# An S5 scan and a Hedgehog attention in one kernel: K's weight in halves, a block of x transposed on TensorE, and a new order of steps

## The chip, the cores and the metric

The kernel runs on one core of a Trainium2 chip. The metric is the device time of one execution in microseconds (us). A core has five engines, each with its own queue of instructions that it takes strictly in order: TensorE (PE; its weight loads are shown apart as PEld), VectorE (DVE), ScalarE (ACT), GpSimd (POOL) and SyncE (SP), which issues transfers. ScalarE and GpSimd issue transfers too. TensorE writes into eight PSUM banks, and VectorE or ScalarE copies ("evacuates") a bank to SBUF before it is used again.

## The reference

From an input x of 2048 tokens by 512 features two branches are computed and mixed by a gate:

```
g = sigmoid((x * gate_w).sum(-1))
# A: a diagonal complex state space with 512 states
h_t = Lam_bar * h_{t-1} + B_bar x_t                a = 2 Re(C h_t) + x * Dskip
# B: linear attention, 32 heads of 16, feature map = softmax(+) beside softmax(-)
q, k, v = x @ wqkv
phi(u) = [softmax(u @ w_phi), softmax(-u @ w_phi)]
b = (phi(q) (phi(k)^T v) / (phi(q) sum(phi(k)) + 1e-6)) @ wo
out = g * a + (1 - g) * b
```

Inputs and output are bf16, and sums are in f32.

## The kernel before

The 2048 tokens are sixteen tiles of 128. Tile `ti` holds the tokens with remainder `ti // 4` modulo 4 within a quarter `ti % 4` of 512 tokens: the scan runs four tokens at a step, so a tile is one phase of one quarter. `xT` holds x with features on partitions; `x_load` (line 224) fills a tile of it by a transposing transfer from HBM on SP's queue, eight tiles first, then B's matrices plain and transposed (`Bn_r`, `Bn_i`, `BrT`, `BiT`), the other eight tiles, Q's weight transposed (`WTq`), C's matrices and `Wo`.

The head-wise map `w_phi` is folded into the weights of K and Q. `st_B` makes a block-diagonal matrix `BD` from `Wc` (w_phi) and a mask. `st_W` (line 278) transposes K's weight on TensorE, four 128 x 128 blocks at a time, into `WTk`; `st_f` multiplies by `BD` and writes K's folded weight `Wk2`. `st_w` does the same for Q.

For each tile, `st_k` and `st_v` are four matmuls each (128 x 128 weights, 512 columns), whose result goes to `Xq` or to one of eight buffers `vx`. For each pair of tiles the feature map follows: `x` (a tree of four maxima and a subtraction), `n` (the same with minima), `e` (two exponentials on ScalarE), `s` (a tree of four sums, then ln and exp on ScalarE, then a product on VectorE). `st_a` accumulates phi(k)^T v in two PSUM banks over all tiles, and the gate's sums with it. For Q the same comes in pairs `A`, `B` and in groups of four tiles, `X1`..`S3`, whose results four transposing transfers on SP bring into `phT`.

The state space: `V`, `U`, `P`, `P2` to `P4`, `M` compute its parameters from three vectors (`vec_n`), which GpSimd loads and TensorE transposes in `V`; `i0`..`i3` make sine and cosine tables, `D` diagonal matrices `dg`, `p` and `g` the inputs of the scan, `z0`..`z3` the scan itself on VectorE (ten steps each), `h`, `c`, `K`, `r`, `b` what the output needs. The output of tile n is `y` (state and direct part), `o` (attention: matmuls, ln and exp on ScalarE, two products on VectorE, a transposing transfer) and `t` (`Wo`, the gate, the store).

All functions `st_*` are generators, and the order of the whole kernel is written out by hand in the string `ORDER` (line 24). Each token runs one generator to its next `yield`. `k1@3` is the first part of `k1` with PSUM bank 3; `W1:D` has its evacuation on VectorE instead of ScalarE; `t4:A` issues its store from ScalarE's queue; `F:36` issues 36 matmuls on a constant tile, whose result nobody reads. The block is a manual schedule for PE, DVE, ACT and SP (line 152): each of them gets its instructions in the order in which the tokens issue them. Waits between engines are added for the data; so are waits for buffers that are used again. GpSimd's order is chosen by the framework.

Of the kernel before, what the change touches and what calls it, by code (L numbers as in the profile page):

```python
# [10 lines left out]
ALU = mybir.AluOpType  # L11
AX = mybir.AxisListType
# [12 lines left out]
B B F:36 W2@0 W2 W1@1 W1:D W0@2 W0:D W3@3 B W3 B F:8 f3@4 F:1 V@5 V f3 f0@6 f2@7 P f0 U P f2 P2 f1@0 U f1 v1@1 P2 v2@2  # L25
k1@3 k0@5 P2 P2 U V2@4 k5@6 k3@7 P P2 P4 P4 U P4 i0 k2@0 P3 P2 P3 k1 i0 k7@3 i1 i0 k0 i0 i0 v1 i2 i1 x0 x0 k4@5 i1 n0
k3 x0 i1 M v2 V2 v7@1 n0 i2 k2 k7 v3@4 i1 i3 x0 n0 x0 i3 k4 k5 v4@7 i2 n0 i2 k6@2 i2 x1 n0 i3 x1 v0@0 i3 D v4 v3 p22@3
x1 n1 v5@5 p00@6 x1 n1 x1 i3 x2 L n1 x2 p30@7 v7:D e0 p20@4 x2 D v5 n1 n1 p10@1 p20 n2 p02@5 p30 p10 x2 e0 D n2 s0 v0
v6@4 k6 g101@7 p00 x2 s0 x3 n2 s0 g001@1 g000@0 n2 s0 e1 e1 g001 n2 s1 s0 s0 e2 g100@2 p22 g101 g001 x3 n3 gw s0 e2 n3
k9@6 x3 v6 g100 a0@31 k9 g000 a0 s1 n3 s1 n3 k8@4 g000 x3 s1 s1 s1 g100 k10@6 s2 k8 x3 n3 p12@0 e3 g101 k11@2 s1 e3 x4  # L30
k11 a1 s2 g010@4 n4 k10 a1 s2 g011@7 n4 x4 s2 n4 x4 n4 s3 g010 g011 s2 x4 s3 x4 n4 x5 k12@2 s3 p02 s2 e4 n5 k13@6 x5
e4 s3 x5 s2 n5 s3 g010 g011 s4 a2 k12 g011 x5 n5 s3 p32@5 k13 s4 n5 a2 s3 x5 n5 x6 g010 z0 s4 w0@2 n6 w0 p32 v9@7 w3@6
z0 g111@4 p12 g210@2 n6 w3 s4 e5 e5 w1@5 s5 w1 a3 v8@0 x6 k14@6 s4 z0 g111 g110@5 a3 n6 z0 v9 s5 v8 k15@7 k14 s4 v11@0
z0 x6 x6 z0 k15 s4 n6 w2@6 g110 w2 g201@7 x6 g111 g111 x7 g110 z0 a4 x7 c01@6 z0 g200@4 g110 z1 s5 q1@5 v11 z1 g311@0
s5 x7 s5 n6 s5 c01 n7 g201 e6 z1 g211@6 a4 z1 g201 x7 g200 v10@7 z1 z1 e6 g200 z0 g210 q0@4 g211 g210 s5 q1 n7 v12@5
q0 q3@4 x7 n7 s6 z0 g210 n7 s6 n7 g211 s6 v10 nA xA g301@2 s6 a5 e7 z1 g300@7 g211 q3 e7 nA v14@6 z1 xA z2 nA q2@4 v14
a5 z2 g300 xA s6 s7 q2 z2 s6 s7 z2 g301 g300 xA s7 g311 g301 v12 g310@6 xA g311 z1 nA c11@4 z1 nA eA z2 nB s7 z2 c03@7
c12@2 g310 xB g311 eA q15@5 c12 s6 c03 s7 g310 h01@0 nB q15 g310 sA c10@2 z2 s7 h01 c11 c13@7 xB nB v13@5 z3 xB h11@6
z2 c10 z3 a6 z2 sA z2 h11 q9@0 c02@4 v13 sA q9 xB a6 nB c13 h10@2 q6@5 c02 v15@0 z3 q12@7 q10@6 q8@4 xB v15 sA nB
h21@0 q12 z3 h00@7 q6 q10 q5@5 eB q8 s7 q4@6 a7 sA eB q4 z3 z3 h10 z3 c00@4 q7@2 c00 a7 sB sA r1 sB z3 sB z3 h20@6 sA  # L40
K0@4 sB q7 sA sB z3 q13@2 q5 h31@5 h21 q14@0 sB G h20 h30@6 sA sB h00 q13 h31 sA sB sB sB G h30 Y q11@2 END N1 K2@7 X1
Y o0@5 N1 o1@6 r0 K0 o1 Y X1 N1 X1 q11 Y o0 X1 N1 o0@3 X1 N1 o0 o1@4 y1@1 o1 q14 o1 o0 b1 o0 N2 y0@2 o2@0 o0 K2 X2 o0
E1 o1 E1 E1 y1 E1 o2 X2 K3@7 N2 X2 o2@5 o1 y0 o1 y2@3 S1 o2 o2 o2 K1@6 K1 y2 S1 o2 S1 N2 X2 o2 S1 y3@4 o3@0 y0 r1 X2
N2 K3 S1 S1 N2 y3 r0 S1 S1 S1 o3 o3@5 o3 G y1 y3 y7@6 o3 E2 t0 y2 o3 E2 E2 E2 G t1 o3 t0 y5@7 t2 N3 y4@0 t2 y7 b1 X3
r3 o4@5 N3 S1 S2 S2 o4 o4@2 y5 b0 o4 o4 t1 o3 y4 o4 o5@3 o5 o4 b0 S1 o5@5 S2 t3 o5 b3 S1 o5 r2 o5 y4 y6@1 t3 r2 o4 y7
o6@2 t1 b2 S2 r3 o6 o6@3 y6 b2 o7@4 o6 S2 t0 o5 y5 y6 o5 t4 o6 b3 o7 S2 S2 t2 y8@5 o6 X3 o6 S2 y11@2 t4 X3 t4:A o7@0
o7 N3 y10@3 X3 o7 o6 N3 y11 t5 y10 X3 N3 o7 t6 o7 S2 E3 y8 S2 o8@4 E3 E3 o8 o8@0 o8 S2 o8 o7 t5:D t6:D o8 o8 y10 y8
y9@7 o10@1 o9@4 E3 o9 S3 o9@0 S2 o9 o10 o8 o9 o9 y9 S3 t7 S3 o9 t6 o10@4 y11 o9 o10 S3 o10 y9 o10 S3 o10 y14@0 t8 t7
y13@1 S3 S3 t5:A o11@4 y12@6 y13 o11 t8 o10 S3 o11@5 o11 t9 S3 t9:D S3 y14 t3:A o11 t10 o12@7 o11 S3 o11 t10:D o12
o12@4 o12 o12 y14 o12 o13@5 S3 o13 o13@3 y12 o12 o13 t7 t8:A o13 o11 o13 o12 o14@7 o14 o14@4 o13 o14 t9:A y13 o14 y12  # L50
o14 o14 o15@5 o15 o15@3 y15@7 o15 o15 t11 o15 t11 o13 o14 o15 y15 t12 y15 t10 t12 t14 t14 o15 t11 t12 t13 t14:A t15
t15 t13:D t15:A t13
# [16 lines left out]
def kernel(  # L69
# [29 lines left out]
    ORD = (3, 1, 0, 2)  # L99
    KVW = 4 * (Dh + 1)  # L100
# [61 lines left out]
    nc.scalar.dma_start(out=wk_nat[:], in_=B_wqkv[:, D:2 * D].rearrange("(k p) n -> p k n", p=P))  # L162
    nc.scalar.dma_start(out=Wc[:], in_=B_w_phi.rearrange("(k hl) e f -> (hl e) k f", hl=8))
    nc.scalar.dma_start(out=Wv[:], in_=B_wqkv[:, 2 * D:3 * D].rearrange("(k p) n -> p k n", p=P))
# [19 lines left out]
    K0T = const.tile([P, KT, D], BF16, name="K0T")  # L184
# [42 lines left out]
    for ti in range(8):  # L227
        x_load(ti)
# [5 lines left out]
    for ti in range(8, NTI):  # L234
        x_load(ti)
# [26 lines left out]
    mask16 = stg.tile([P, 8], F32, name="mask16", bufs=1)  # L262
    nc.vector.tensor_reduce(out=mask16[:], in_=identf[:].rearrange("p (g e) -> p g e", e=16), axis=AX.X, op=ALU.add)
# [13 lines left out]
    def st_W(j):  # L277
        pt = bank([P, KT, P], BF16, "ptw")
        for dtile in range(KT):
            nc.tensor.transpose(pt[:, dtile, :], wk_nat[:, dtile, j * P:(j + 1) * P], ident[:])  # L280
        yield
        evac(WTk[:, j, :], pt[:].rearrange("p a b -> p (a b)"))
        yield
# [143 lines left out]
    def tile_mm(pt, ti, W):  # L427
        for kt in range(KT):
            MM(out=pt[:], lhsT=xT[:, kt, ti * P:(ti + 1) * P], rhs=W[:, kt, :], start=(kt == 0), stop=(kt == KT - 1))  # L429

    def st_k(ti):
        pk = bank([P, D], F32, "pk")
        tile_mm(pk, ti, Wk2)
        yield
        evac(Xq[:, ti, :], pk[:])
        yield

    def st_v(ti):
        pv = bank([P, D], F32, "pv")
        tile_mm(pv, ti, Wv)  # L440
        yield
        evac(vxb[ti % NVX][:, :, 0:Dh], pv[:].rearrange("p (h e) -> p h e", e=Dh))
        yield
# [77 lines left out]
    def st_a(n):  # L521
        for u in range(2):
            ti = 2 * n + u
            if ti == 0:
                live["acc"] = [bank([P, 512], F32, f"kvacc{b}") for b in range(2)]
            for m in range(NB):
                MM(out=acc(m), lhsT=live["EE", n][:, u, m].rearrange("p s f -> p (s f)"),  # L527
                   rhs=vxb[ti % NVX][:, 4 * m:4 * m + 4, :].rearrange("p h e -> p (h e)"),
                   start=(ti == 0 and m % 4 == 0), stop=(ti == NTI - 1), skip_group_check=True)
            for kt in range(KT):  # L530
                MM(out=live["acc"][1][:, 4 * KVW + ti:4 * KVW + ti + 1], lhsT=xT[:, kt, ti * P:(ti + 1) * P],
                   rhs=gw_b[:, kt:kt + 1], start=False, stop=(ti == NTI - 1 and kt == KT - 1), skip_group_check=True)
            yield
# [123 lines left out]
    def st_r(j):  # L657
        for a, k0 in enumerate((DG_LR, DG_NLI)):
            if sel["eng"] == "act":
                nc.scalar.mul(out=c3buf(j, a), in_=C2r[:, j, :], mul=dgs[:, k0, j:j + 1])  # L660
            else:
                VS(out=c3buf(j, a), in0=C2r[:, j, :], scalar1=dgs[:, k0, j:j + 1], scalar2=None, op0=ALU.mult)
            yield
# [163 lines left out]
```

## Time and profile before

| | |
|---|---|
| time, median of 3 runs | 167.73 us (167.42 to 168.08) |
| profiled execution, first to last instruction | 166.1 us (the page gives no other time for it) |
| PE busy | 157.6 us (95%) |
| VectorE busy | 143.7 us (87%) |
| ScalarE busy | 114.8 us (69%) |
| GpSimd busy | 9.6 us (6%) |
| mean granted TensorE clock | 0.994 |
| x tile by transposing transfer, issue to landing | 3.9 us (median of 16) |

The times of the profile are measured from the first instruction. In a timeline a row gives the start, the time taken, the engine, the line of the code, the operation, output and inputs, the shape and the number of instructions. In brackets stands the idle time of the engine before it and what ended it. A step's cost to its engine is the distance from its start to the next start, which may be shorter than its own time.

### The profile page before, as it was taken

What the parts mean: (1) busy time and instruction counts of PE and PEld (TensorE: products, weight loads), DVE (VectorE), ACT (ScalarE), POOL (GpSimd) and SP (SyncE); (2) the same over time, 40 slices, a digit from 0 to 9 for tenths busy, and PEclk for the clock granted to TensorE, in tenths of its full rate; (3) what the DMA queues carried; (4) which work ended last, traced back from release to release, by engine and by line L of the source; (5) the groups of instructions that cost most, each with busy time, mean ns of one, the idle gap of its engine ahead of it and who ended that gap; (6) DMA issues with size and microseconds to landing.
All of it is one profiled execution on the core that took longest, in us unless ns stands there. A gap on an engine that the chain in (4) does not pass through costs nothing.

```text
span 166.1 us, 3051 instructions
## 1 busy us (share of the span) xinstructions
PE 157.6 (95%) x1088; PEld 82.3 (50%) x1109; DVE 143.7 (87%) x354; ACT 114.8 (69%) x236; POOL 9.6 (6%) x28
## 2 busy tenths in 40 slices
PE   7689999999999999999999999999999999999990
PEld 7444455455465454454454554545446445445440
DVE  4379999999999999999999999999999996818410
ACT  3389999999898268578965966876888356423331
POOL 8218200000000000000000000000000000000000
PEclk9999999999999999999999999999999999999997
DMA  4969945464444200000000019212296585478542
GB/s 111 267 121 281 142 99 97 95 98 95 95 105 85 98 0 6 0 0 0 0 4 0 0 24 181 52 32 63 65 132 154 162 189 129 119 174 216 128 125 95
DMA packets 50830, 15.94 MB, mean 96 GB/s; under 512 B 46208, under 2 KB 50816, under 8 KB 50816
## 3 DMA queue, kind: packets, MB, share of 16 engines
q1 hardware_dynamic: 48064, 13.77, 39.8%
q10 hardware_dynamic: 2592, 1.98, 4.4%
q8 instruction: 8, 0.13, 0.3%
q14 instruction: 6, 0.05, 0.1%
q0 software_dynamic: 160, 0.01, 0.1%
HBM read 2.64 MB, written 2.10 MB: 29 GB/s over the span
## 4 chain that ended last, share of the span: by engine, by line
PE 84%; DVE 8%; DMA 3%; POOL 2%; issue 1%; ACT 1%; POOLq 0%
PE pgq L552 8%; PE py L750 8%; PE pgq L555 8%; PE py L705 8%; PE pq L429 8%; PE py L706 8%; PE pv L429 5%; PE py L712 4%; PE pk L429 4%; DMA vec_n<-in_A_log_dt_dram 3%; PE kvacc L527 3%; PE pn L728 3%; PE pk L674 2%; PE pk L675 2%; DVE psi L406 2%; DVE mxk L464 1%
## 5 line engine op out<-in xcount | busy, mean ns | idle before, releaser
L429 PEld LDWEIGHTS <-xT 128*128 128x128 bf16 x192 | 18.1, 97 | 20.8 <-DMA xT<-in_A_x_dram 0.7
L136 ACT ACTIVATE EEk<-EEk 128x1024 bf16<-128x1024 bf16 x20 | 21.0, 1070 | 0.8 <-DVE EEk L480 0.8
L737 DVE SCALAR_TENSOR_TENSOR on<-pn,RG,rd 128x256 bf16<-128x256 f32 x32 | 14.4, 474 | 3.2 <-ACT rd L136 1.7
L429 PE MATMUL pv<-Wv,xT 128*128 128x512 bf16 x62 | 16.0, 379 | 0.3 <-DMA xT<-in_A_x_dram 0.2
L750 PE MATMUL py<-Wo,oT 128*128 128x512 bf16 x62 | 15.8, 379 | 0.1
L555 PE MATMUL pgq<-xT,LBT 128*128 128x512 bf16 x60 | 15.5, 379 | 0.2
L429 PE MATMUL pq<-Wq,xT 128*128 128x512 bf16 x61 | 15.6, 379 | 0.1
L429 PE MATMUL pk<-Wk,xT 128*128 128x512 bf16 x61 | 15.1, 379 | 0.2
L136 ACT ACTIVATE EEq<-EEq 128x1024 bf16<-128x1024 bf16 x12 | 11.8, 1044 | 3.3 <-DVE EEq L480 3.3
L136 ACT ACTIVATE ld<-pn 128x16 f32<-128x16 f32 x32 | 4.7, 182 | 12.6 <-PE pn L728 12.6
L706 PE MATMUL py<-Wv,H 128*128 128x512 bf16 x31 | 11.7, 379 | 0.1
L705 PE MATMUL py<-Wk,H 128*128 128x512 bf16 x31 | 11.7, 379 | 0.1
L705 PE MATMUL py<-C2r,H 128*128 128x512 bf16 x31 | 11.7, 379 | 0.0
L117 ACT CAST Xq<-pq 128x512 bf16<-128x512 f32 x16 | 9.2, 589 | 3.6 <-PE pq L429 3.4
L117 ACT CAST uv<-pgq 128x512 bf16<-128x512 f32 x16 | 9.3, 588 | 3.4 <-PE pgq L560 2.3
L706 PE MATMUL py<-C2i,H 128*128 128x512 bf16 x30 | 11.4, 379 | 0.1
L756 DVE TENSOR_SCALAR ot<-py,G 128x512 bf16<-128x512 f32 x5 | 3.7, 747 | 8.4 <-PE py L750 8.4
L117 ACT CAST vx<-pv 128x512 bf16<-128x512 f32 x15 | 8.7, 598 | 2.6 <-PE pv L429 2.6
L754 ACT ACTIVATE ot<-py,G 128x512 bf16<-128x512 f32 x11 | 7.4, 678 | 4.5 <-PE py L750 4.5
L117 ACT CAST Xq<-pk 128x512 bf16<-128x512 f32 x16 | 9.2, 601 | 1.4 <-PE pk L429 1.4
L464 DVE TENSOR_TENSOR smk<-smk 128x512 bf16<-128x512 bf16 (+2 forms) x30 | 9.8, 327 | 0.0
L500 DVE TENSOR_TENSOR EEk<-EEk,rck 128x2048 bf16<-128x2048 bf16 x8 | 9.7, 1214 | 0.0
(179 smaller groups left out, 348.6 us busy)
## 6 DMA issues: line engine op xcount, KB each, us to landing
out_dram<-ot SPq DMA_DIRECT2D x9, 128.0 KB, 2.1
out_dram<-ot ACTq DMA_DIRECT2D x7, 128.0 KB, 2.1
C2r<-in_B_wqkv_dram ACTq DMA_DIRECT2D x1, 512.0 KB, 4.4
Wv<-in_B_wqkv_dram ACTq DMA_DIRECT2D x1, 512.0 KB, 5.9
Bn_r<-in_A_B_re_dram SPq DMA_DIRECT2D x1, 512.0 KB, 5.1
Bn_i<-in_A_B_im_dram SPq DMA_DIRECT2D x1, 512.0 KB, 6.0
Wo<-in_B_wo_dram SPq DMA_DIRECT2D x1, 512.0 KB, 3.8
xT<-in_A_x_dram SPq DMA_TRANSPOSE x16, 3.9
```

Of the source, the lines that this page charges most:

```text
L117: nc.scalar.copy(out=out_ap, in_=in_ap)
L136: ins = nc.scalar.activation(**kw)
L429: MM(out=pt[:], lhsT=xT[:, kt, ti * P:(ti + 1) * P], rhs=W[:, kt, :], start=(kt == 0), stop=(kt == KT - 1))
L464: VT(out=t[:], in0=cur[:, :, :, 0:n, :], in1=cur[:, :, :, n:2 * n, :], op=op)
L500: VT(out=E5, in0=E5, in1=rc[:].to_broadcast([P, L, 2 * NB, Dh, 4]), op=ALU.mult)
L552: MM(out=pgq[:], lhsT=BT[:, kt, js], rhs=xT[:, kt, r1 * NC:(r1 + 1) * NC], start=(kt == 0), stop=False)
L555: MM(out=pgq[:], lhsT=LBT_[:, kt, js], rhs=xT[:, kt, (r1 - 1) * NC:r1 * NC], start=False, stop=(r1 == 1 and kt == KT - 1))
L705: MM(out=py[:], lhsT=src[:, j, 0, off:off + P], rhs=cr[:, j, :], start=(j == 0), stop=False)
L706: MM(out=py[:], lhsT=src[:, j, 1, off:off + P], rhs=ci[:, j, :], start=False, stop=False)
L737: nc.vector.scalar_tensor_tensor(out=on[:, 2 * hf:2 * hf + 2].rearrange("p g h e -> p (g h) e"), in0=pns[hf][:, :, 0:Dh], scalar=RG[:, ti: ...
L750: MM(out=py[:], lhsT=oT[:, g, :], rhs=Wo[:, g, :], start=False, stop=(g == HG - 1))
L754: nc.scalar.mul(out=ot[:], in_=py[:], mul=G[:, ti:ti + 1])
```

## The change

K's weight is loaded as two transfers of two row blocks each instead of one of four. An untransposed block of x, the first 512 tokens (tiles 0, 4, 8 and 12), is loaded into `xn` (the memory of `K0T`, which is written late) in two transfers behind it on ScalarE's queue. `Wc` and `Wv` move from ScalarE's queue to SP's; `Wv` is issued behind a two-column memset of its tile, which stands behind the mask's reduction on VectorE. TensorE transposes the block's four tiles in a new step `T`; the other twelve x tiles are loaded as before, six ahead of B's matrices and six behind them. `st_W` now takes one row block of K's weight at a time and writes a column block of `WTk`, so a fold `f` needs only the `W` of its own number. `BD` is made by one instruction of VectorE instead of four, with a bf16 mask. K's and V's tiles go in the order `KORD`. The list `ORDER` is new from the first to the last token: the same steps otherwise, one block of 40 fill matmuls instead of 36, 8 and 1.

```diff
 ORDER = """
-B B F:36 W2@0 W2 W1@1 W1:D W0@2 W0:D W3@3 B W3 B F:8 f3@4 F:1 V@5 V f3 f0@6 f2@7 P f0 U P f2 P2 f1@0 U f1 v1@1 P2 v2@2
-k1@3 k0@5 P2 P2 U V2@4 k5@6 k3@7 P P2 P4 P4 U P4 i0 k2@0 P3 P2 P3 k1 i0 k7@3 i1 i0 k0 i0 i0 v1 i2 i1 x0 x0 k4@5 i1 n0
-k3 x0 i1 M v2 V2 v7@1 n0 i2 k2 k7 v3@4 i1 i3 x0 n0 x0 i3 k4 k5 v4@7 i2 n0 i2 k6@2 i2 x1 n0 i3 x1 v0@0 i3 D v4 v3 p22@3
-x1 n1 v5@5 p00@6 x1 n1 x1 i3 x2 L n1 x2 p30@7 v7:D e0 p20@4 x2 D v5 n1 n1 p10@1 p20 n2 p02@5 p30 p10 x2 e0 D n2 s0 v0
...
-y13@1 S3 S3 t5:A o11@4 y12@6 y13 o11 t8 o10 S3 o11@5 o11 t9 S3 t9:D S3 y14 t3:A o11 t10 o12@7 o11 S3 o11 t10:D o12
-o12@4 o12 o12 y14 o12 o13@5 S3 o13 o13@3 y12 o12 o13 t7 t8:A o13 o11 o13 o12 o14@7 o14 o14@4 o13 o14 t9:A y13 o14 y12
-o14 o14 o15@5 o15 o15@3 y15@7 o15 o15 t11 o15 t11 o13 o14 o15 y15 t12 y15 t10 t12 t14 t14 o15 t11 t12 t13 t14:A t15
-t15 t13:D t15:A t13
+B F:40 W1@0 W1:D W0@1 W2@2 W2 W3@3 W0:D f1@4 f1 W3:D f0@5 f0 T1@6 T1:D f2@7 f2 f3@0 f3:D T3@1 T2@2 T2 T0@3 T0:D k1@4
+V@6 V T3 U U P U U P P2 P2 P2 P2 P2 P4 k0@5 P4 v1@7 k1 k4@0 k0 P4 i1 i1 P k5@2 P2 i1 i1 i1 P3 k4 v1 P3 M i2 i2 i2 k2@3
+k2 x0 x0 x0 k3@1 k3 i0 i0 v7@6 k5 n0 n0 n0 i3 i3 i0 i0 x1 i3 v7 i3 v4@4 x0 v4 k7@5 x1 n0 k9@0 x0 k9 i3 i0 i2 n1 V2@7
+k7 x2 D v5@3 v5 x1 D i2 x1 x1 k8@1 k6@2 k6 v2@6 v2 n0 x2 x2 p10@4 p10 x2 x2 n1 n1 p00@0 p00 D v6@5 p30@3 p30 v6 p02@2
+p20@6 n2 n1 n2 n2 n2 n2 v0@4 n3 n3 x3 n1 v3@0 g100@3 n3 n3 x3 g000@5 p20 g000 g100 x3 x3 p02 L e0 k8 x4 x4 V2 e0 s0 s0
...
+y2 S1 S1 S1 S1 o3@6 o2 o2 o3 o3@3 o3 o3 y3 r0 S1 S1 N2 o2 E2 E2 y1@1 y1 o1 o1 o1 G t0 y7@0 y7 y7 E2 y5@4 o3 S1 S1 S1
...
+S2 o7@5 o7 t6 X3 X3 o7@2 b2 b2 S2 S2 b3 y11 o8@4 o7 o8 o8@6 o8 o7 o8 y10 y10 N3 N3 t6 N3 N3 N3 E3 E3 E3 y9@1 o8 o9@4
+o8 o7 o7 y14@6 o9 o9@5 y13@2 o9 o9 o9 o9 y9 y9 E3 S3 o7 t0:A t3:A o10@4 o10 o10@5 o10 y13 t7 S3 t5:A o10 y14 o9 o8 S3
+S3 t2 o10 o10 S3 o10 S3 S3 S3 y8@4 t7:D t7:A y8 y8 t9 t1 o11@5 o11 o11@0 o11 o11 o11 S3 S3 S3 t8 t8 y13 y12@5 y12 o11
+o11 t9:D o13@0 S3 o13 o13@4 y12 o13 o13 o13 o13 t4:A o13 t10 o14@1 o14 o14@0 o14 o14 y11 t8:A t10:D o12@4 o14 o14 o12
+o12@3 o12 o12 o12 t9 y14 o12 t11 o15@1 o15 o15@0 o15 o14 o15 o15 t13 o12 y15@4 o15 t11:D t14 t14:D t14:A t13 y15 o15
+t12 y15 t12:D t15 t15 t15:A t10 t6 t13 t11 t12
 """
+    KORD = (0, 4, 8, 12, 1, 5, 2, 6, 3, 7, 9, 13, 10, 14, 11, 15)
-    nc.scalar.dma_start(out=wk_nat[:], in_=B_wqkv[:, D:2 * D].rearrange("(k p) n -> p k n", p=P))
-    nc.scalar.dma_start(out=Wc[:], in_=B_w_phi.rearrange("(k hl) e f -> (hl e) k f", hl=8))
-    nc.scalar.dma_start(out=Wv[:], in_=B_wqkv[:, 2 * D:3 * D].rearrange("(k p) n -> p k n", p=P))
+    K0T = const.tile([P, KT, D], BF16, name="K0T")
+    xn = K0T
+    for k0 in (0, 2):
+        nc.scalar.dma_start(out=wk_nat[:, k0:k0 + 2, :], in_=B_wqkv[k0 * P:(k0 + 2) * P, D:2 * D].rearrange("(k p) n -> p k n", p=P))
+    for r0 in (0, 2):
+        nc.scalar.dma_start(out=xn[:, r0:r0 + 2, :], in_=x2[0:4 * P].rearrange("(c r) d -> c r d", r=4)[:, r0:r0 + 2, :])
+    nc.sync.dma_start(out=Wc[:], in_=B_w_phi.rearrange("(k hl) e f -> (hl e) k f", hl=8))
...
-    for ti in range(8):
+    make_identity(nc, ident[:])
+    identf = stg.tile([P, P], F32, name="identf", bufs=1)
+    make_identity(nc, identf[:])
+    mask16 = stg.tile([P, 8], BF16, name="mask16", bufs=1)
+    nc.vector.tensor_reduce(out=mask16[:], in_=identf[:].rearrange("p (g e) -> p g e", e=16), axis=AX.X, op=ALU.max)
+    nc.vector.memset(Wv[:, 0, 0:2], 0.0)
+    nc.sync.dma_start(out=Wv[:], in_=B_wqkv[:, 2 * D:3 * D].rearrange("(k p) n -> p k n", p=P))
+    for ti in KORD[4:10]:
         x_load(ti)
...
-    for ti in range(8, NTI):
+    for ti in KORD[10:]:
         x_load(ti)
...
     def st_W(j):
         pt = bank([P, KT, P], BF16, "ptw")
-        for dtile in range(KT):
-            nc.tensor.transpose(pt[:, dtile, :], wk_nat[:, dtile, j * P:(j + 1) * P], ident[:])
-        yield
-        evac(WTk[:, j, :], pt[:].rearrange("p a b -> p (a b)"))
+        for k in range(KT):
+            nc.tensor.transpose(pt[:, k, :], wk_nat[:, j, k * P:(k + 1) * P], ident[:])
+        yield
+        evac(WTk[:, :, j * P:(j + 1) * P], pt[:])
+        yield
+
+    def st_T(r):
+        pt = bank([P, KT, P], BF16, "ptx")
+        for kt in range(KT):
+            nc.tensor.transpose(pt[:, kt, :], xn[:, r, kt * P:(kt + 1) * P], ident[:])
+        yield
+        evac(xT[:, :, KORD[r] * P:(KORD[r] + 1) * P], pt[:])
         yield
...
     def st_B():
-        for kt in range(HG):
-            VT(out=BD[:, kt, :].rearrange("p (g f) -> p g f", f=Dh), in0=Wc[:, kt, :].unsqueeze(1).to_broadcast([P, 8, Dh]),
-               in1=mask16[:].unsqueeze(2).to_broadcast([P, 8, Dh]), op=ALU.mult)
-            yield
+        VT(out=BD[:].rearrange("p k (g f) -> p k g f", f=Dh), in0=Wc[:].unsqueeze(2).to_broadcast([P, HG, 8, Dh]),
+           in1=mask16[:].unsqueeze(1).unsqueeze(3).to_broadcast([P, HG, 8, Dh]), op=ALU.mult)
+        yield
...
-    def st_k(ti):
+    def st_k(n):
         pk = bank([P, D], F32, "pk")
-        tile_mm(pk, ti, Wk2)
+        tile_mm(pk, KORD[n], Wk2)
         yield
-        evac(Xq[:, ti, :], pk[:])
+        evac(Xq[:, n, :], pk[:])
         yield
```

`st_v` and `st_a` take their tiles through `KORD` in the same way.

## The prediction, made before the changed kernel was run

> **What bounds the kernel now.** I read the page's first two parts, then the busy time by stretch, then the timeline of VectorE, then the chain that ended last.
>
> ```profile
> span 166.1 us, 3051 instructions
> ...
> PE 157.6 (95%) x1088; PEld 82.3 (50%) x1109; DVE 143.7 (87%) x354; ACT 114.8 (69%) x236; POOL 9.6 (6%) x28
> ...
> PE   7689999999999999999999999999999999999990
> ...
> DVE  4379999999999999999999999999999996818410
> ```
>
> ```profile
> 10.00:45.00 35.00, 34.54 (x211) 17.24 (x214) 34.70 (x102) 34.12 (x63) 5.25 (x14) 1.00 0.66 125
> 45.00:135.00 90.00, 89.36 (x626) 45.87 (x636) 89.93 (x198) 64.41 (x134) 0.00 (x0) 1.00 0.28 58
> 135.00:163.00 28.00, 26.95 (x176) 13.26 (x178) 15.02 (x29) 12.52 (x36) 0.00 (x0) 1.00 0.61 153
> ```
>
> The columns after the stretch's length are the busy times of PE, PEld, DVE, ACT and POOL, then the granted clock. Two engines are full at once: from 10 to 135 us PE works 123.9 of 125 us and VectorE 124.6. PE stays full until its last matmul. So a shorter PE start is worth something only if VectorE can follow, and a longer VectorE costs at once. ScalarE is full until 45 us only.
>
> The timeline of VectorE shows what one step costs there, from its start to the next start:
>
> ```profile
> 14.43 0.46 DVE L464 TENSOR_TENSOR mxk<-Xq 128x512 bf16<-128x512 bf16 x1
> 14.93 0.29 DVE L464 TENSOR_TENSOR mxk<-mxk 128x256 bf16<-128x256 bf16 x1
> 15.14 0.42 DVE L464 TENSOR_TENSOR mnk<-Xq 128x512 bf16<-128x512 bf16 x1
> ...
> 19.66 0.41 DVE L464 TENSOR_TENSOR mxk<-Xq 128x512 bf16<-128x512 bf16 x1
> 20.00 0.68 DVE L480 TENSOR_TENSOR EEk<-mnk,Xq 128x1024 bf16<-128x1024 bf16 x1
> 20.60 0.28 DVE L464 TENSOR_TENSOR mxk<-mxk 128x256 bf16<-128x256 bf16 x1
> ```
>
> At 19.66 a tree's first step (x2) is followed by foreign work, which starts 0.34 later, before the 0.41 is over. At 14.43 the same step (x0) is followed by its own reader, which starts only at 14.93: 0.50, the whole 0.46 and 0.03 more. I call a step that stands directly behind the one whose output it reads *chained*. The list of before has ten chained pairs on VectorE, and each starts 0.034 after its forerunner's end, where a stranger starts about 0.08 before it: five in the parameter chain (0.20 against 0.08), x0, n1 (0.215 against 0.102), x6, S2 and S3. The price is 0.079 to 0.163 a pair, 0.113 on average.
>
> The start and the end:
>
> ```profile
> 5.20 1.07 PE L280 MATMUL ptw<-ident,C2r 128*128 128x128 bf16 x16 [0.64 <-DMA C2r<-in_B_wqkv_dram]
> ...
> 8.89 0.16 PE L287 MATMUL pvt<-ident,vec_n 12*128 12x12 bf16 x1 [0.87 <-DMA vec_n<-in_A_log_dt_dram]
> ...
> 9.10 0.17 DVE L289 CAST vec<-pvt 128x12 f32<-128x12 bf16 x1 [1.40 <-PE pvt L287]
> ```
>
> ```profile
> 160.05 2.12 PE py L750 x9
> 162.20 0.69 ACT ot L754
> ```
>
> VectorE's full stretch begins with the cast of vec (ends 9.26), and PE's last matmul ends at 162.17. Behind it lie 3.95 us (ScalarE's scaling, the last store, the end) to the span's 166.11. The page gives no other time of this execution; the median of the three runs, 167.73, lies 1.62 above its span. My sum is made in the span's times, and 1.62 is added at the end.
>
> **The start, part by part.** The fill matmuls go from 45 to 40 in one block: 3.45 us for 36, so 40 end at 1.11 + 40 x 0.096 = 4.95. K's weight arrives in halves of 256 KB issued at about 0.8 and 1.3 on ScalarE's queue; a 128 KB store lands in 2.1, the 512 KB Wo in 3.8, so the halves are there by 2.9 to 5.1, under the fill. x's block follows in two more issues at 1.8 and 2.3 (0.53 each) and lands between 3.9 (2.1 later) and 7.4 (5.1 later, as Bn_r in a crowded queue); T1 wants the first half at about 6.5, T3 the second at 7.2: at most 0.4 late. The Wv load waits on SP for a memset behind the mask's reduction (3.5 us by the rows of before); queued behind it are six x transposes, Bn, BrT and BiT. SP issues four x transposes fewer (4 x 1.33 = 5.3) and two plain loads more (2 x 0.55), so the first x tile lands near 9 instead of 5, used at 12 at the earliest, and the BrT transposes start at 12.7 + 0.5, used from 26 on: cost nothing. On POOL the identities only move ahead of iota; the five vector loads keep their sum, so vec_n lands near 8.8 again. BD is one instruction of about 0.6 for four of 0.28; VectorE takes it before W1's copy, so Wc, which now leads SP's queue, must be there: at 2.9 to 5.6 by the same 2.1 and its own 4.8, wanted at 4.7, so up to 0.9 late. The tile order (KORD) renames which x tile a step takes and changes no duration.
>
> PE: four W blocks end at 6.0 (16 transposes in 1.07), and the folds follow as their copies finish; ScalarE copies W2, f1, f0, f2 from 5.85 at 0.5 each, the last done near 8.3, while VectorE takes W1, W0, W3, T1 (0.37 each) and f3. So k1 starts near 8.4, with all transposes of x but no wait for its loads. PE then goes through the rest of its list without a hole. The added 16 transposes are 1.07. Summing the durations of the rows over PE's list, k1's start to the end is 151.8: PE alone would end at 160.2, 1.9 earlier than now. Vec's transposition stands behind k1 (0.86), so the cast of vec ends near 9.7: 0.4 later than before. Bounds: 9.1 (as early as vec_n allowed before) to 11.0 (Wc and x both late: 0.9 + 0.4).
>
> **VectorE, the part that decides.** From the cast of vec to the last product of the last feature group (S3, whose four blocks the end waits for) the trace of before takes 145.29 - 9.26 = 136.03. The new list has the same VectorE steps in this stretch but three evacuations that ScalarE takes over (v7, t5, t6): -0.60 - 2 x 0.67 = -1.94. It holds 101 chained pairs instead of 10. They are the runs of one name, as "x0 x0 x0", "s1 s1 s1" or "N3 N3 N3", with nothing of VectorE between: 53 in the trees of max and min, 27 in those of the sums, 11 in the parameter chain, 5 in the tables, 5 in the scan steps. Each kind priced by its own duration plus 0.034 less its start-to-start time gives 11.46; before has 1.13 of it, so +10.33. The wait for E3's four exponentials between N3 and S3 (4 x 0.95 + 0.3, beside 2.3 of other work) and the one for rho add up to 2.4 where before lost 1.9: +0.5. Together 144.9, so S3 ends at 9.7 + 144.9 = 154.6 instead of 145.3.
>
> What is late next: PE's list takes block o13 when the second of S3's transposed blocks has landed: 1.3 for the first's issue, 2.8 for the landing (the medians of SP's phT transposes), 0.1: 158.8. From there PE has o13, o14, o12, o15 (0.26 each) and twelve groups of four matmuls (0.863 each), 11.4: **the last matmul ends at 170.2**. Other crossings come out alike. Scan 3 ends at 105.6 and PE has 63.2 from its reader h31 on: 168.9. S1 ends at 127.3, lands at 130.2, and 39.2 follow: 169.4. The same sums for the list of before give 162.3 as the largest path, against 162.17 in the trace, and VectorE's sum stays within 1.2 of the trace at every point up to 130 us. So PE's waits are spread: some 2.9 before p10 at 21, 1.6 before a0, 1.0 before a2, 2.3 before a7, the rest later. ScalarE is no limit: its sum reaches e0 at 29.4, and VectorE wants it at 34.5; the k evacuations are 3 to 10 ahead of the trees.
>
> Sum: 170.2 + 3.95 + 1.62 = **175.8**, 8.1 above the median.
>
> The unknown in it is the price of a pair. By the two ends of the rows, 101 x 0.079 = 8.0 or 101 x 0.163 = 16.5 against 11.46: -3.5 or +5.0. Below nothing is excluded, since a reader can't start before its writer's end. I take the price by kind, since nine of the ten pairs lie at 0.111 to 0.119 in it; 0.163 counts one slow first step. With the cast of vec (-0.6 to +1.3) and up to 3 for waits that feed each other, the forecast alone reaches from 172 to 179.
>
> **Rivals.** *Chained steps cost nothing.* The trees' steps would then run at 0.335, 0.20 and 0.14 whoever follows, VectorE's 11.46 vanish, and PE would be late once, by 0.6 before p10: last matmul 160.9, time 166.5, faster by 1.2. For it speaks that the new list fits its two engines together at just these prices; against it that every one of the ten pairs shows the 0.034. It decides where a pair costs under some 0.03: there the new paths fall to 162.2. Chance 0.10. The Trainium skill's page "VectorE: DVE Perf Modes", section "The DRAIN you can't avoid", speaks for this rival: every VectorE instruction is flushed whatever follows, and "the semaphore costs nothing extra here". By that rule the time is the rival's 166.5; the trace disagrees, 0.34 for a step with a stranger behind it and 0.50 with its reader.
>
> *Part of it is hidden.* Where VectorE would have had to wait anyway, a pair costs less: half of the 10.33 gone would be 170.6. Against it: the sums leave VectorE no hole before N3. Chance 0.14.
>
> *The late VectorE drags the others.* ScalarE stands behind an exponential that waits for a tree, the evacuations of k and g queue behind it, PE waits for banks, and the trees for k: another 3 to 5, so 179 to 181. For it: ScalarE is full up to 45 us now. Against: those evacuations are 3 to 10 ahead. Chance 0.10.
>
> *The start gains more or less*: it only moves the cast of vec, and is in the ranges.
>
> **How the numbers follow.** Forecast 0.62 (172 to 179, at 175.8); half hidden 0.14 (168.5 to 172); dragging 0.10 (over 179); costless pairs 0.10 (166.5); in between, within 0.5% of before, 0.04. Half a per cent, 0.8 us, is about what a measurement of this kernel can tell from no change. Faster 0.10, same 0.04, slower 0.86. The range leaves out the costless pairs, no change and the worst half of the dragging, 0.19 in all: 168.5 to 180.5.
>
> **What would show it.** Right: VectorE's trees in the new profile go at 0.50, 0.32 and 0.25 a step in runs; VectorE is full from about 10 to 140; PE's idle time, by waits, comes from VectorE's EEk, H and dg and sums to some 8 to 10; k1's first matmul starts near 8.4; S3's last product ends near 154.6. Wrong: trees at 0.34, PE without holes, and a last matmul near 161; or waits of VectorE for ScalarE or PE between 20 and 130 us.

## The result: 1.083 times the time of before, 6 us above the forecast

| | before | after |
|---|---|---|
| median of the runs (us) | 167.91 (167.42 to 168.39) | 181.72 (181.38 to 182.75) |
| span of the profiled execution | 166.1 | 181.0 |
| cast of vec ends | 9.26 | 14.78 |
| last product of S3 ends | 145.29 | 160.53 |
| between these two | 136.03 | 145.75 |
| PE's last matmul ends | 162.17 | 177.10 |

The ratio is 1.0834, with a 95% interval of 1.0794 to 1.0873. The forecast was 175.8, in a range of 168.5 to 180.5: the sign is right, and the time lies 1.2 above the range. The profiled execution of after took 182.75, the longest of its four, 1.0 above their median, which matters where a reading below is compared with a median. Executions that came over 1.5% above their kernel's fastest are left out of the times below.

The first two parts of the page of after:

```profile
span 181.0 us, 3093 instructions
...
PE 164.1 (91%) x1120; PEld 84.3 (47%) x1120; DVE 153.0 (85%) x356; ACT 115.3 (64%) x236; POOL 9.9 (5%) x28
...
PE   7469996996999999999999799999799999999991
...
DVE  3336999999999999999999999999999996954650
```

And its busy time by stretch (columns as before: PE, PEld, DVE, ACT, POOL, granted clock, DMA share, GB/s):

```profile
10.00:45.00 35.00, 29.98 (x171) 14.93 (x172) 29.89 (x91) 27.43 (x50) 5.54 (x14) 0.95 0.65 126
45.00:135.00 90.00, 86.61 (x599) 43.35 (x596) 87.99 (x188) 65.32 (x127) 0.00 (x0) 0.98 0.15 35
135.00:178.00 43.00, 41.35 (x283) 20.36 (x280) 31.25 (x58) 19.30 (x57) 0.00 (x0) 1.00 0.71 152
```

Both engines have lost their full first stretch: until 45 us PE works 30.0 of 35 us where it had worked 34.5, and VectorE 29.9 instead of 34.7. From 16 us on VectorE is full and PE is the one with holes. The chain that ended last says the same in one line, before and after:

```profile
PE 84%; DVE 8%; DMA 3%; POOL 2%; issue 1%; ACT 1%; POOLq 0%
```

```profile
DVE 58%; PE 27%; DMA 6%; issue 3%; ACT 3%; ACTq 1%; DVEq 0%
```

The timeline of VectorE shows the runs of one name at the price that the forecast had put on them. One tree of sums, and the foreign step behind it:

```profile
48.40 0.68 DVE L477 TENSOR_TENSOR smk<-EEk 128x1024 bf16<-128x1024 bf16 x1
49.12 1.08 DVE L477 TENSOR_TENSOR smk<-smk 128x512 bf16<-128x512 bf16 x3
50.11 0.28 DVE L477 TENSOR_TENSOR mnk<-mnk 128x256 bf16<-128x256 bf16 x1
```

The second level starts 0.04 after the end of the first, at 49.12, and the four levels take 1.71 us up to the next instruction's start. Over the whole trace 100 pairs are chained, with a median price of 0.120 us and 11.8 us in all; in before they were 10 with 1.16.

What the forecast had not seen is the start, from the timelines of PE and VectorE:

```profile
8.95 0.40 PE L294 MATMUL ptx<-ident,K0T 128*128 128x128 bf16 x4 [2.50 <-DMA K0T<-in_A_x_dram]
...
11.29 1.46 PE L294 MATMUL ptx<-ident,K0T 128*128 128x128 bf16 x12 [1.49 <-DMA K0T<-in_A_x_dram]
12.54 1.91 PE L442 MATMUL pk<-Wk,xT 128*128 128x512 bf16 x4
14.39 0.18 PE L301 MATMUL pvt<-ident,vec_n 12*128 12x12 bf16 x1
...
14.61 0.17 DVE L303 CAST vec<-pvt 128x12 f32<-128x12 bf16 x1 [1.39 <-PE pvt L301]
```

T1 waits 2.50 us for the first half of x's block and T3 1.49 for the second. Behind them in PE's order stand k1 and vec's transposition. k1's four matmuls take 1.91 us, where four of the same shape take 1.04 elsewhere, as PE's granted clock is 0.66 between 10 and 13 us. So VectorE's long stretch begins 5.5 us later than before. The list of DMA issues up to 14 us has the reason's first half (the last column is the median time from issue to landing):

```profile
C2r<-in_B_wqkv_dram ACTq DMA_DIRECT2D x2, 256.0 KB, 3.9
K0T<-in_A_x_dram ACTq DMA_DIRECT2D x2, 256.0 KB, 7.9
Wv<-in_B_wqkv_dram SPq DMA_DIRECT2D x1, 512.0 KB, 9.0
...
vec_n<-in_A_log_dt_dram POOLq DMA_DIRECT2D x1, 1.0 KB, 8.4
```

x's halves, issued at 1.89 and 2.41, need 7.9 us where the halves of K's weight, the same size, need 3.9. The vectors are late too: the last of vec_n's three loads lands at 11.81, in before at 8.76. PE comes to them later still, so no wait shows it, but with x in time and these loads as they were the cast could not have ended before about 12. The end is as it was, the last matmul and ScalarE's scaling by the chain:

```profile
176.22 0.88 PE py L764 x4
177.12 0.69 ACT ot L768
```

### The profile page after: what moved, and what is told of

Read it like the earlier page. It is cut to its first block, busy times and chain, and to the rows that moved or that the text cites. A ratio compares the mean times of both kernels' runs of the same rounds, so it can differ in the third digit from the quotient of the medians.

```text
span 181.0 us, 3093 instructions
## 1 busy us (share of the span) xinstructions
PE 164.1 (91%) x1120; PEld 84.3 (47%) x1120; DVE 153.0 (85%) x356; ACT 115.3 (64%) x236; POOL 9.9 (5%) x28
## 4 chain that ended last, share of the span: by engine, by line
DVE 58%; PE 27%; DMA 6%; issue 3%; ACT 3%; ACTq 1%; DVEq 0%
DVE smk L477 7%; DMA K0T<-in_A_x_dram 5%; DVE mxk L477 5%; DVE mnk L477 4%; DVE EEk L513 4%; DVE smq L477 4%; PE pq L442 4%; PE py L764 4%; DVE w L618 4%; DVE EEk L493 3%; DVE EEk L487 3%; PE py L726 3%; DVE on L751 3%; PE pk L442 2%; ACT EEq L137 2%
## 5 line engine op out<-in xcount | busy, mean ns | idle before, releaser
L442 PEld LDWEIGHTS <-xT 128*128 128x128 bf16 x192 | 18.7, 100 | 22.4 <-issue 3.4
L751 DVE SCALAR_TENSOR_TENSOR on<-pn,RG,rd 128x256 bf16<-128x256 f32 x32 | 13.9, 474 | 7.1 <-ACT rd L137 7.0
L442 PE MATMUL pk<-Wk,xT 128*128 128x512 bf16 x64 | 17.4, 411 | 0.0
L442 PE MATMUL pv<-Wv,xT 128*128 128x512 bf16 x64 | 16.7, 393 | 0.1
L442 PE MATMUL pq<-Wq,xT 128*128 128x512 bf16 x64 | 16.1, 378 | 0.4 <-ACT Xq L118 0.4
L720 PE MATMUL py<-C2i,H 128*128 128x512 bf16 x32 | 12.1, 379 | 0.0
L768 ACT ACTIVATE ot<-py,G 128x512 bf16<-128x512 f32 x10 | 6.8, 682 | 7.5 <-PE py L764 4.2
L618 DVE TENSOR_TENSOR_SCAN w<-ssm_par,ut 128x512 bf16<-128x512 f32 x8 | 9.5, 1213 | 0.0
L720 PEld LDWEIGHTS <-H 128*128 128x128 bf16 x64 | 6.2, 97 | 6.9 <-issue 1.0
L118 ACT CAST vx<-pv 128x512 bf16<-128x512 f32 x16 | 9.4, 599 | 0.0
```

Of the source, the lines that this page charges most:

```text
L618: nc.vector.tensor_tensor_scan(out=w[:, ri, :], data0=rb, data1=ut[:, ri, :], initial=0.0, op0=ALU.mult, op1=ALU.add)
L720: MM(out=py[:], lhsT=src[:, j, 1, off:off + P], rhs=ci[:, j, :], start=False, stop=False)
L751: nc.vector.scalar_tensor_tensor(out=on[:, 2 * hf:2 * hf + 2].rearrange("p g h e -> p (g h) e"), in0=pns[hf][:, :, 0:Dh], scalar=RG[:, ti: ...
L768: nc.scalar.mul(out=ot[:], in_=py[:], mul=G[:, ti:ti + 1])
```

## The experiments

Theory: two separate causes. (1) The list's chained pairs on VectorE cost about 10 us. (2) The start is late, because x's block lands late. Rivals: a pair costs nothing, or something behind the pairs holds the time up anyway; the late start alone is the cause, or is hidden.

**The list with few chained pairs.** The kernel after with 62 entries moved, for example

```
-P4 i1 i1 P k5@2 P2 i1 i1 i1 P3
+P4 i1 x0 i1 P k5@2 P2 i1 x0 i1 i1 P3
...
-M i2 i2 i2 k2@3 k2 x0 x0 x0 k3@1
+M i2 x0 i2 i2 k2@3 k2 k3@1
```

> The kernel after, with 62 entries of its step list moved a few places, so that 19 instead of 100 neighbours on VectorE have the second read what the first wrote; tiles, loads and all other steps stay, and so does VectorE's work. Theory (a chained pair costs 0.12 us more, the median of the trace of after): VectorE loses 81 x 0.12 = 9.7 us of the stretch from vec's cast to S3's last product (145.75 us in the trace of after, so about 136), and the time falls by as much, from 181.7 to about 172.0 (bounds 170 to 173.5, because a neighbour that is 0.079 or 0.163 costs 81 times as much). PE alone, from k1 at 12.54, needs 151.8 and would end at 164.3, so that the time can't be under about 169. Rival 1 (chained steps cost nothing, VectorE is late for another reason that the list brings): S3's last product stays at 160.5 and the time at 181 to 182. Rival 2 (the late start and the clock drop, not VectorE, set the end): the VectorE stretch shortens, but the time stays over 178.

Measured: 178.32 (178.07 to 179.44), ratio to before 1.0647 (1.0591 to 1.0703). The price of the pairs did go, from 11.8 to 2.1 us. But VectorE's stretch fell only from 145.75 to 143.25, and the time by 3.4, far from the 172 of the theory; by its words this is the second rival's outcome. Not even all of the 3.4 is the list's: in the profiled execution the cast ends at 11.48, 3.3 earlier than in that of after, though nothing at the start was touched. VectorE now stands still for 8.9 us in the stretch (2.8 in after). Some of the waits of VectorE, with total, number and longest:

```profile
DVE smq L476 <- ACT EEq L136: 1.7, 1, 1.7
...
DVE mnk L476 <- ACT Xq L117: 1.3, 1, 1.3
...
DVE smk L476 <- ACT EEk L136: 0.8, 2, 0.4
```

None of these three is among VectorE's waits in after. By this run alone, either a second bound lies close below, or the moves made new waits: a tree that is mixed with a stranger finishes later, and ScalarE's exponentials, which wait for it, start later. The run can't tell them apart. A later one does.

**Chained pairs put into the kernel before**, with its start and loads untouched:

```
-i3 x0 n0 x0 i3 k4 k5 v4@7 i2 n0 i2
+i3 x0 x0 n0 k4 k5 v4@7 i2 n0 i3 i2
...
```

> The kernel before, its start, loads and tiles unchanged, with entries of its step list moved a few places so that about 50 instead of 10 neighbours on VectorE are chained. Theory (0.12 us a pair): VectorE gets 40 x 0.12 = 4.8 us longer, from 136.0 to 140.8 us between vec's cast and S3's last product. Before the change VectorE's own bound lies at about 166.5 and PE's at 167.9, so that some 1.4 of it is hidden: about 171.3 (bounds 169.5 to 172.7). Rival (a pair costs nothing): 167.9, and VectorE's stretch stays at 136.

Measured: 173.54 (172.90 to 175.05), ratio 1.0355 (1.0277 to 1.0434). 50 pairs are chained, their price rose by 4.61 (0.115 for each of the 40 new ones), and the stretch by 5.36. The time rose by 5.8, above the expected bounds: nothing of it was hidden, though I had reckoned with 1.4 of slack. The chain that ended last went from PE to VectorE:

```profile
DVE 64%; PE 22%; issue 4%; ACT 3%; DMA 3%; POOL 1%; DVEq 0%; POOLq 0%
```

So chained pairs make even the old kernel slower, and "they cost nothing" (167.9) is out.

**vec's steps ahead of x's second half**, in the kernel after:

```
-f3:D T3@1 T2@2 T2 T0@3 T0:D k1@4 V@6 V T3 U U P U U P P2 P2 P2 P2 P2 P4 k0@5 P4 v1@7
+f3:D V@6 V U U P U U P P2 P2 P2 P2 P2 P4 P4 T3@1 T2@2 T2 T0@3 T0:D k1@4 T3 k0@5 v1@7
```

> The kernel after, with vec's transposes, its cast and VectorE's short steps behind it (V, U, P, P2, two of P4) ahead of T3 in the step list, so that on PE and VectorE they stand behind the first half of x's block only and not behind the second. Theory (VectorE's long stretch starts when vec's cast ends, and that was at 14.78 because the cast stood behind x's second half and k1): the cast ends at about 10.7, 4 us earlier, S3's last product at about 156.5, and the time is about 177.9 (bounds 176.9 to 179). Rival (the start is hidden by later waits, for example because EEk waits for k tiles that come no earlier): the cast ends earlier, but VectorE idles until k1's features and the time stays at 181 to 182.

Measured: 180.46 (179.07 to 181.32), ratio 1.0749 (1.0683 to 1.0816). In the profiled execution the cast ends at 10.87 and S3's last product at 156.71, both as expected (10.7 and 156.5), with a stretch of 145.84. What the cast's transposition waits for now is not x but vec's own loads (2.18 us on PE, until 10.50). The time fell by only 1.3, where 3.8 were expected, and the intervals of the two ratios overlap. From one profiled execution to the other it fell by 2.7, for the median execution of after is 1.0 shorter than its profiled one. Most of what is missing then lies behind S3: 21.7 us from there to the end of the span, where after has 20.5. There the traces show transfers on SP's queue. S3's first transposing transfer is issued 1.47 us after S3's last product (0.14 in after), and PE waits 0.42 for a transposed block of S3 and 0.38 for the last tile of the attention's output, where PE waits for no transfer behind S3 in after.

**Wv behind x on one queue**, in the kernel after:

```
-    nc.vector.memset(Wv[:, 0, 0:2], 0.0)
-    nc.sync.dma_start(out=Wv[:], in_=B_wqkv[:, 2 * D:3 * D]...)
...
+    nc.scalar.dma_start(out=Wv[:], in_=B_wqkv[:, 2 * D:3 * D]...)   # behind x's two halves
```

> The kernel after, with Wv's load (512 KB) moved from SP's queue ahead of the x transposes to ScalarE's queue behind x's two halves, and without the memset that held it back. Two theories on why x's halves took 7.9 us from issue to landing. A (Wv's load, issued at 2.23 and landing after 9.0 us, shared the DMA engines with them): x's first half lands at about 6.5 and T3's at 7.5, vec's cast ends at about 10, and the time is about 177 (176 to 178.5). B (the x transposes on SP's queue are what slows them, and now start even earlier): x lands at 9 to 12 as before or later, and the time is 181 to 184.

Measured: 179.87 (178.65 to 180.43), ratio 1.0712 (1.0656 to 1.0768). The DMA issues up to 14 us:

```profile
C2r<-in_B_wqkv_dram ACTq DMA_DIRECT2D x2, 256.0 KB, 3.3
K0T<-in_A_x_dram ACTq DMA_DIRECT2D x2, 256.0 KB, 4.6
Wv<-in_B_wqkv_dram ACTq DMA_DIRECT2D x1, 512.0 KB, 5.3
```

x's halves land after 4.6 us instead of 7.9, although the six x transposes on SP's queue now start 1.4 us earlier. T1 no longer waits, T3 waits 0.18, and the cast ends at 10.35. So theory A holds: Wv's load beside them slowed x's halves, and the transposes did not make the difference. The load of vec that landed after 8.4 us in after lands after 4.2 here. Other profiled executions with Wv beside x had 6.2, 6.4, 6.5 and 7.4, so the lateness varies from one execution to the next; 4.5 and 4.6 are the two with Wv behind. The time was expected to be 177 (176 to 178.5) and missed that; it fell by 1.9. Of the 4.4 us that the cast gained over the profiled execution of after, 2.1 are lost again behind S3, where PE waits 0.36 for a block of S3 and 1.34 for the attention's last tile.

**The list without the start.** The kernel after with the loads of before and no T steps:

```
-    for k0 in (0, 2): ...            # K's weight in halves
-    for r0 in (0, 2): ...            # x's block
-    nc.sync.dma_start(out=Wc[:], ...)
+    nc.scalar.dma_start(out=wk_nat[:], ...)
+    nc.scalar.dma_start(out=Wc[:], ...)
+    nc.scalar.dma_start(out=Wv[:], ...)
...
-    for ti in KORD[4:10]:
+    for ti in KORD[0:10]:
...
-T1@6 T1:D ... T3@1 T2@2 T2 T0@3 T0:D ... T3
```

> The kernel after with the loads of before: K's weight whole, Wc and Wv on ScalarE's queue, every x tile by SP's transposes (ten of them ahead of B's loads), no steps T0 to T3; the step list and the tile order of after stay. It shows the list without the start. Theory (start and list add up: in the traces vec's cast ends 5.5 us later and VectorE's stretch from there to S3's last product is 9.7 us longer): vec's cast at about 9.5, S3's last product at 9.5 + 145.7 = 155.2, and with the 21.2 us that lie behind it in the median of after the time is about 176.4 (bounds 175 to 178). Rival (the list costs only because the late start shifts everything against each other): under 171.

Measured: 178.00 (177.52 to 178.37), ratio 1.0576 (1.0517 to 1.0634). The cast ends at 10.25, the stretch is 145.65, S3's last product ends at 155.91.

**The start without the list.** The kernel after with the list of before from the first k tile on:

```
+B F:40 W1@0 W1:D W0@1 W2@2 W2 W3@3 W0:D f1@4 f1 W3:D f0@5 f0 T1@6 T1:D f2@7 f2 f3@0 f3:D T3@1
+T2@2 T2 T0@4 T0:D k1@3 V@6 V T3 P U P P2 k0@5 U
 P2 P2 P2 U V2@4 k5@6 k3@7 v1@1 ...   # from here the list of before, v1 and v2 later
```

> The kernel after, its loads, T steps and tile order, with the step list of before from the first k and v tiles on (k ahead of v at the very start, since Wv lands late); it shows the start without the list. Theory (they add up): vec's cast at 11.0 to 14.8, as in the traces so far, VectorE's stretch 136 as in before, S3's last product at 147 to 151, and the time 168.5 to 173, about 171. Rival (before's list hides a late start, for PE has other work at first): 167.5 to 168.5. Second rival (the late start alone makes the 14 us): over 178.

Measured: 172.06 (171.17 to 172.47), ratio 1.0217 (1.0148 to 1.0286). The cast ends at 12.61, the stretch is 136.66. The list alone costs 10.0 us and the start alone 4.1, together 14.2, against 13.8 for the change. The two parts add up, and the list is the larger. (The start holds the order up to the first k tiles, with the cast of vec behind k1.)

**The dependence taken away, the order kept.** To see what in the list costs the 10 us, levels two to four of each tree read the tree's own input. They do the same work in the same sizes on other data, so the kernel's result changes:

```
             VT(out=t[:], in0=cur[:, :, :, 0:n, :], in1=cur[:, :, :, n:2 * n, :], op=op)
-            cur = t
```

> The kernel after with one line less: levels two to four of every tree (max, min and sum of 16 features) read the tree's input instead of the level before, in the same sizes, so that the output is not the reference's. No instruction is moved and none is shorter by its form; about 66 of the 100 chained neighbours on VectorE are no longer chained, and no neighbour has come between them (which is how it differs from the run that moved entries of the list). Theory 1 (the chained pairs themselves cost the list's 10 us): VectorE's stretch shrinks by 66 x 0.12 = 7.9 us from 145.7 to 137.8, and the time is about 174 (bounds 172.5 to 175.5). Theory 2 (a second bound lies 3 us below, in waits between ScalarE, PE and VectorE that the list holds anyhow, as the run with moved entries would have it): VectorE waits in place of the pairs, and the time is 178 to 179.5. In that case the gaps on VectorE grow by 5 us or more; by theory 1 they stay near 2.8.

Measured: 173.84 (172.60 to 174.63), ratio 1.0358 (1.0298 to 1.0418), against 174 by theory 1. The stretch is 137.78, as worked out (137.8). VectorE's gaps in it are 3.1, near the 2.8 of after, so theory 2's waits did not come. The same tree of sums as above:

```profile
43.32 1.42 DVE L477 TENSOR_TENSOR smk<-EEk 128x1024 bf16<-128x1024 bf16 x4
44.66 0.28 DVE L477 TENSOR_TENSOR mnk<-Xq 128x256 bf16<-128x256 bf16 x1
```

Four levels in 1.34 us up to the next start, instead of 1.71. And PE has much of its work back; the first row owes part of it to an earlier cast in this execution (12.01):

```profile
10.00:45.00 35.00, 33.21 (x202) 16.95 (x207) 32.75 (x102) 31.80 (x57) 9.08 (x14) 1.00 0.64 134
45.00:135.00 90.00, 87.97 (x619) 45.13 (x630) 88.84 (x194) 66.93 (x136) 0.00 (x0) 1.00 0.23 45
```

This also settles the first run: its new waits came with its moves.

**The control: the same line taken from the kernel before.**

> The same line taken from the kernel before (levels two to four of each tree read the tree's input; the output is not the reference's), as the control of the run beside it: of its 10 chained pairs most lie outside the trees, so that the edit should change nothing here. By either theory 167.3 to 168.2, VectorE's stretch 135.5 to 136.1. If it is faster by over 1 us, the edit itself makes the trees cheaper, and the run beside it can't be read as the price of chaining.

Measured: 167.60, ratio 0.9984 (0.9968 to 1.0000), stretch 135.78. The edit by itself is worth some 0.3, at most 0.5 by the interval, so the 7.9 us above are the dependence, with the wait that goes with it; the runs don't part these two.

**Both causes taken away together.**

> Both suspected causes taken from the kernel after: the trees' levels read the tree's input (the output is not the reference's), and Wv's load stands behind x on ScalarE's queue. Theory 1 (late start and chained pairs are all that makes it slower): vec's cast at about 10.4, VectorE's stretch 137.8, S3's last product at about 148.2, and the time 169.5 to 172, not under 168, since PE alone from k1 needs 151.8 us. Theory 2 (a second bound in the list): 176 to 178.

Measured: 171.29 (171.12 to 171.57), ratio 1.0217 (1.0197 to 1.0236). The cast ends at 10.26, the stretch is 137.62, S3's last product ends at 147.89. That is inside theory 1's range. What is left to before is 3.4 us by the medians and 3.3 by the spans: 1.0 in the cast, 1.6 in the stretch, and 0.7 behind it. The stretch still holds some 34 chained pairs, 2.7 us above before's price; less the 1.9 of the evacuations that ScalarE took, they account for half of the 1.6. The other half was not followed up.

**Towards a faster kernel.** Two runs take from the change what could help the kernel before. First vec's loads ahead of the identities on GpSimd's queue:

```
+    for n, src in enumerate((A_Lambda_im, A_Lambda_re, A_log_dt)):
+        nc.gpsimd.dma_start(out=vec_n[4 * n:4 * n + 4, :], ...)      # right behind the tile's allocation
...
     make_identity(nc, ident[:])
...
-    (the same three loads, behind the second identity)
```

> The kernel before with one edit: GpSimd issues the three loads of vec ahead of the two identities instead of behind them. In the trace of before PE waits 0.87 us for the last of them and VectorE 1.40 us for the cast behind it. Theory (that wait stands on the path, since both engines are full from there on): vec's loads land about 1.1 us earlier, the cast ends at about 8.3 instead of 9.26, and the time falls by 0.9 to about 166.9. Rival (PE's next steps wait for f's evacuations or x's tiles instead): 167.5 to 168.

Measured: 167.29 over 12 runs (167.03 to 167.69), ratio 0.9946 (0.9917 to 0.9975). This beats both kernels, by 0.66 us over before (0.9 was expected; the cast ends at 8.57, not 8.3). The wait for vec in the timelines fell from 0.87 to 0.18 on PE and from 1.40 to 0.70 on VectorE:

```profile
8.20 0.16 PE L288 MATMUL pvt<-ident,vec_n 12*128 12x12 bf16 x1 [0.18 <-DMA vec_n<-in_A_log_dt_dram]
...
8.40 0.17 DVE L290 CAST vec<-pvt 128x12 f32<-128x12 bf16 x1 [0.70 <-PE pvt L288]
```

Then, on top of it, K's weight in halves with its transposes by row blocks and BD in one step, x's tiles all by SP's transposes:

```
-    nc.scalar.dma_start(out=wk_nat[:], ...)
-    nc.scalar.dma_start(out=Wc[:], ...)
+    nc.scalar.dma_start(out=wk_nat[:, 0:2, :], ...)
+    nc.scalar.dma_start(out=Wc[:], ...)
+    nc.scalar.dma_start(out=wk_nat[:, 2:4, :], ...)
...
-B B F:36 W2@0 W2 W1@1 W1:D W0@2 W0:D W3@3 B W3 B F:8 f3@4 F:1 V@5 V f3 f0@6 f2@7 P f0 U P f2 P2 f1@0 U f1
+B F:40 W1@0 W1:D W0@1 W2@2 W2 W3@3 W0:D f1@4 f1 W3:D f0@6 f0 f2@7 f2 f3@0 V@5 f3:D V P U P P2 U
```

> The kernel before with vec's loads first as in the run beside it, and of the change only K's weight in halves, transposed and folded by row blocks as they land (W0 and W1 from the first half), Wc between the halves and BD in one step; x by SP's transposes and the rest of the list as before. In the trace of after K's weight lands 0.6 us earlier and PE ends its last fold at about 7.3, where before it ended at 9.7. Theory (the folds are what the first k and v tiles wait for): PE starts on them at about 8.0 to 8.5, 1.2 to 1.7 earlier, vec's cast ends at 8.0 to 8.5, and the time is 165.8 to 166.8. Rival (Wv, now third on the queue, or x's transposes end the wait instead): as vec first alone, 166.9, or no gain, 167.8.

Measured: 168.19, ratio 1.0019 (0.9985 to 1.0054), the rival's outcome, and worse than vec first alone. The expectation had misread the trace of after: there the last fold ends at 9.80, not 7.3, and only the first half of K's weight lands earlier than in before (4.56 against 5.15), the second at 5.34. The folds end earlier, at 8.6, but the first v tile then waits for its weight:

```profile
9.93 1.89 PE L429 MATMUL pv<-Wv,xT 128*128 128x512 bf16 x7 [1.19 <-DMA Wv<-in_B_wqkv_dram]
```

## Why the forecast had the sign and missed the size

**Chained pairs: right, in mechanism and in size.** The forecast said 101 pairs at 0.113 on average, 10.33 more than before. One of them turned out not to be chained, the median is 0.120, and the stretch is 145.75 where 144.9 was worked out, 0.85 more. The run that only removes the dependence gives back 7.9 us for some 66 pairs. With a stranger behind it a step overlaps the next by some 0.08 us, and with its reader behind it, it does not. The Trainium skill's page "VectorE: DVE Perf Modes", section "The DRAIN you can't avoid", states from a measurement of eight copies that the semaphore between them costs nothing extra. That does not hold for the steps here, at 0.12 us a pair.

**The step that failed: "x's block ... lands between 3.9 ... and 7.4 ...: at most 0.4 late".** T1 started at 8.95 instead of about 6.5, and T3 at 11.29 instead of 7.2. I had taken 5.1 us, the landing of a 512 KB load in a crowded queue, as the upper end. In the profile it was 7.0 for the first half and 8.8 for the second. Two things were missed. I had Wv's load wait on SP for a memset until 3.5 us, a time from the rows of before. But the change moves the identities, from which the mask is made, ahead of GpSimd's iota: the mask's reduction starts at 1.83 instead of 3.76, and Wv was issued at 2.23, ahead of x's second half. And I had not counted Wv's 512 KB, on another queue, as work in front of x's 512 KB at all. With Wv behind x on one queue the halves land after 4.6, inside my bounds. The Trainium skill's page "DMA: Bandwidth & Descriptors", section "Queues, rings and completion order", says that each DMA engine takes turns, packet by packet, between the queues that have work for it; the two landing times, 7.9 us beside Wv and 4.6 ahead of it, agree with that.

**"vec_n lands near 8.8 again" failed with it.** It landed at 11.81, and with Wv's load behind x 4.2 us after its issue instead of 8.4. Behind the late k1 this cost nothing in after; in the run with vec's steps ahead of T3 it was the wait that set the cast.

**k1 near 8.4 and the cast near 9.7: wrong by consequence,** at 12.54 and 14.78. The cast stands behind k1 on PE, so the late block moved the whole VectorE stretch. That is 5.1 of the 6.85 us by which the span exceeded the forecast's 174.15; the stretch adds 0.85, and 0.9 is lost behind S3 (block o13 starts 5.0 after S3's last product, not 4.2). Of the 5.1, some 1.5 belong to PE's lower clock in this execution, which the forecast had not reckoned with: the last twelve transposes take 1.46 and k1 1.91, where they take 0.84 and 1.03 in the run with the levels cut. And the last step of the forecast's path was not the one that bound: o13 did not wait for S3's second block, which had landed at 165.19, 0.35 before. From 158.4, where it waited 0.26 for a product of VectorE for an earlier output, PE has no hole to its end. By medians the start alone costs 4.1, where I had 0.4: 3.7 of the 5.9 by which the median lies above the forecast.

**The small terms of the start were right.** The fill ends at 4.93 (forecast 4.95), and Wc lands at 4.36. K's first half is there under the fill, at 4.56; the second lands 0.4 after its end, at 5.34, and still the W blocks run from 4.77 to 6.0, as forecast.

**PE's idle time: right in sum, roughly so in place.** From k1 to the last matmul PE idles 7.85 us (forecast 8 to 10). The longest wait, 1.9, is the one before p10 that the forecast put at 2.9. The view names ScalarE's evacuation into vx as its end, at 28.89, but VectorE's dg, which the forecast meant, was ready only at 28.75. Next come 1.8 for a0 (1.6 in the forecast), 1.1 for a product of the attention's output and 1.0 for a later accumulation, all on VectorE.

**The rivals.** "Chained steps cost nothing" and "part of it is hidden" fell with the run that chained before and the one that cut the levels. "The late VectorE drags the others" came nearest to the time, with 179 to 181, but not to its mechanism: between 20 and 130 us VectorE waits for nobody by more than 0.12 us at once. "The start only moves the cast of vec, and is in the ranges" had the path right; its range, 9.1 to 11.0, was too narrow by 3.8.

## What to carry to other kernels

Count which instructions of one engine stand directly behind the one whose output they read, and price each by start-to-start times of the trace: 0.12 us on some 100 small steps made 10 us here. But look out before breaking such a run with a stranger where another engine waits for the run's end: in the first run here new waits gave back most of it. When a load must land early, count every byte issued before or beside it on any queue; and ask what the engine's order puts behind the load's reader, here the short step that released the other engine's whole stretch.

## What the runs showed of the hardware that was not expected

PE's granted clock fell after a short hole. In after PE waited 1.8 us up to 44.3 us, and from 45 to 48 us it ran at half the clock. A wait of 1.9 us between 25 and 30 us was followed by no such fall:

```profile
25.00:30.00 5.00, 3.08 (x20) 1.61 (x18) 4.93 (x15) 5.00 (x11) 0.56 (x1) 1.00 0.43 95
30.00:35.00 5.00, 5.00 (x31) 2.86 (x30) 4.79 (x14) 4.97 (x9) 0.00 (x0) 1.00 0.42 89
```

```profile
40.00:45.00 5.00, 3.19 (x37) 1.64 (x36) 4.90 (x16) 3.38 (x7) 0.27 (x1) 1.00 0.58 82
45.00:48.00 3.00, 3.00 (x14) 1.12 (x11) 2.93 (x8) 2.97 (x7) 0.00 (x0) 0.51 0.50 111
```

Behind the waits for x it fell too, to 0.66 from 10 to 13 us and 0.77 from 13 to 16. So a wait of PE can cost more than its own length here; what decides whether it does, the runs don't show. The fall is not what made the change slow, though: of the four executions of after, one with a mean granted clock of 1.000 took 181.38 us, the profiled one with 0.981 took 182.75.

The time from issue to landing of the same 256 KB load, in kernels whose first loads are the same, was 6.2 to 7.9 us from one profiled execution to another when a 512 KB load ran beside it. A start that hangs on such a load is uncertain by more than a microsecond.
